# Letting a list scheduler overlap consecutive VectorE and ScalarE instructions in its model

## The chip, the cores and the metric

One core of one Trainium2 chip. The metric is the time of one execution on the device in microseconds (us). "Waits" of TensorE below are stretches in which TensorE could not start its next matmul; TensorE is the engine that sets the end of this kernel.

## The reference, cut to what matters

```python
def _attn_ref(q, k, v):                      # 4 batches, 8 heads, 768 tokens, head width 64
    k_sum = k.reshape(B, H, nb, 32, D).max(axis=3)      # block maxima of the keys
    v_sum = v.reshape(B, H, nb, 32, D).mean(axis=3)     # block means of the values
    # local scores inside a window of 16 tokens to each side, and scores against k_sum
    ...
    a = np.exp(scores_all); a = a / (np.sum(a, axis=-1, keepdims=True) + 1e-09)
    return np.matmul(a, np.concatenate([v, v_sum], axis=2))

def _moe_ref(x, w_gate, w1, w2):             # 3072 tokens, width 512, 8 experts, hidden 1024
    P = np.exp(x @ w_gate - ...)
    for _ in range(8):                       # Sinkhorn
        P /= P.sum(1, keepdims=True) + 1e-09; P /= P.sum(0, keepdims=True) + 1e-09; P *= N / E
    for e in range(E):
        out += P[:, e:e + 1] * (np.maximum(x @ w1[e], 0.0) @ w2[e])
```

## The kernel before

The kernel does the attention for 16 pairs of heads, 12 to 15 belonging to the last batch; between these it runs expert 0 on whatever tokens are ready, and then runs experts 1 to 7, with fewer and larger products (a Strassen-like scheme). So there are two stages: an attention stage to about 120 us, mixed with the products of expert 0, and an expert stage, in pure form from about 164 us to the end.

The order of all instructions on all engines comes from a list scheduler that runs while the program is being built. Each piece of work is a unit with an engine, a modelled cost, its dependences and a priority. On the chip each engine takes its instructions in just this order and waits at semaphores.

```python
class Plan:
    HOP = 0.15                                   # from one engine to another
    ...
    def order(self):
        ...
        while left:
            best = {}
            for u in left:
                ...
                for e, cost in u.eng.items():
                    t = max([t0, free.get(e, 0.0)]
                            + [d.end + d.lag + (self.HOP if d.on != e else 0.0) for d in u.deps])
                    best.setdefault(e, []).append((t, u, cost))
            for e, c in best.items():
                t_min = min(t for t, _, _ in c)
                t, u, cost = min((x for x in c if x[0] <= t_min + 0.02), key=lambda x: x[1].prio)
                picks.append((t, t + cost, e, u, cost))
            t, end, e, u, cost = min(picks, key=lambda x: x[:2])
            ...
            u.start, u.end, u.on = t, end, e
            free[e] = end
```

The 0.02 in the middle is a tie window: of the units that could start within 0.02 us of the earliest, the one of highest priority is taken.

The softmax here doesn't subtract the row's maximum and nothing guards it: scores larger than these inputs give would overflow.

## Time and profile before

| before | |
|---|---|
| median of the first three executions | 666.17 us (666.14 to 666.85) |
| span of the profiled execution | 664.1 us |
| TensorE waits that the view of waits shows, 17 to 164 us | none |
| hidden TensorE waits, 17 to 164 us (see below) | 0.61 us |

A matmul is drawn from its start to a modelled end: 379 ns for 512 columns, while in an unbroken stream the next one starts 216 ns after it. A wait of less than the difference, 163 ns, is covered by the drawn matmul, and the view of waits does not have it. So in all kernels of this study I measured hidden waits in one way: for every matmul that started 5 to 75 ns after the semaphore that it waited for was raised, the start-to-start time from the matmul before it, less the smallest such time of the same pair of kinds of matmuls in the traces of all kernels.

### The profile page before, as it was taken

How to read it: one execution, taken by the hardware profiler on the slowest of the kernel's cores; microseconds unless marked ns; L12 is line 12 of the kernel's file. 1: busy time of each engine (PE TensorE's matmuls, PEld its weight loads, DVE VectorE, ACT ScalarE, POOL GpSimd, SP SyncE). 2: the span in 40 equal slices, each digit the busy share in tenths (PEclk: the TensorE clock that was granted, in tenths of full speed). 3: DMA queues.
4: the chain of work that ended last, by engine and by line, in shares of the span. 5: the costliest groups of instructions: out<-in, count | busy, mean ns of one | idle time of the engine just before them, and what ended most of it. 6: DMA issues, size and time to landing. Idle time of an engine off the chain costs nothing.

```text
span 664.1 us, 13257 instructions
## 1 busy us (share of the span) xinstructions
PE 656.6 (99%) x5131; PEld 435.9 (66%) x5132; DVE 550.1 (83%) x1036; ACT 410.9 (62%) x769; POOL 199.0 (30%) x257
## 2 busy tenths in 40 slices
PE   8999999999999999999999999999999999999997
PEld 4666666545766666666666666666666666666666
DVE  7899897799988887887779877988778877988776
ACT  6677676556885566556665665555655656556652
POOL 8899522100132222212322222223122213222123
PEclk9999999999999999999999999999999999999999
DMA  9999932700953747373754665373838465335656
GB/s 167 181 145 145 143 70 43 128 1 2 157 96 65 126 75 118 64 128 65 110 97 71 121 91 101 64 127 65 127 64 135 73 96 96 64 64 112 157 134 202
DMA packets 112558, 67.89 MB, mean 102 GB/s; under 512 B 77936, under 2 KB 90480, under 8 KB 112496
## 3 DMA queue, kind: packets, MB, share of 16 engines
q0 software_dynamic: 94816, 57.46, 64.9%
q1 hardware_dynamic: 17152, 9.58, 5.9%
q8 instruction: 40, 0.66, 0.4%
q14 instruction: 22, 0.18, 0.1%
q10 hardware_dynamic: 528, 0.02, 0.0%
HBM read 52.45 MB, written 6.29 MB: 88 GB/s over the span
## 4 chain that ended last, share of the span: by engine, by line
PE 96%; DVE 3%; DMA 1%; issue 0%; ACT 0%; POOLq 0%; DVEq 0%
PE yps L815 22%; PE pA L764 22%; PE pY L815 17%; PE pQ L764 11%; PE hps L211 6%; PE yps L216 6%; PE pR L764 5%; PE sg L347 1%; DMA qst<-in_q_dram 1%; PE av L512 1%; PE vs L357 1%; PE tkq L303 1%; PE av L435 1%; DVE xs L543 1%; PE ss L461 1%; PE av L441 1%
## 5 line engine op out<-in xcount | busy, mean ns | idle before, releaser
L815 PEld LDWEIGHTS <-h 128*128 128x128 f16 x2352 | 230.1, 98 | 88.5 <-issue 1.0
L843 POOL DMA_DIRECT2D out_acc<-y x120 | 101.7, 891 | 372.1 <-ACT y L839 110.3
L839 ACT ACTIVATE y<-pY,P_sb 128x256 f32<-128x256 f32 x168 | 79.8, 477 | 123.3 <-PE pY L815 121.6
L830 DVE SCALAR_TENSOR_TENSOR out_acc<-yps,P_sb,out_acc 128x512 f32<-128x512 f32 x128 | 95.1, 744 | 29.0 <-PE yps L815 29.0
L798 DVE TENSOR_TENSOR h<-h 128x1024 f16<-128x1024 f16 x168 | 109.3, 683 | 1.4
L815 PE MATMUL pY<-w,h 128*128 128x256 f16 x672 | 100.0, 273 | 0.6 <-ACT y L839 0.6
L815 PE MATMUL yps<-w2sum,h 128*128 128x256 f16 x672 | 98.4, 273 | 0.0
L764 PE MATMUL pA<-xT,w 128*128 128x512 f16 x336 | 98.3, 379 | 0.0
L815 PE MATMUL yps<-w,h 128*128 128x256 f16 x672 | 93.3, 273 | 0.0
L830 DVE SCALAR_TENSOR_TENSOR out_acc<-pY,P_sb,out_acc 128x512 f32<-128x512 f32 x84 | 62.8, 748 | 29.1 <-PE pY L815 27.4
L764 PEld LDWEIGHTS <-w 128*128 128x128 f16 x672 | 65.8, 98 | 31.6 <-issue 0.2
L764 PEld LDWEIGHTS <-w1sum 128*128 128x128 f16 x504 | 49.3, 98 | 45.0
L786 DVE CUSTOM_DVE_ANT_0 h<-pQ,snap 128x512 f16<-128x512 f32 x84 | 57.6, 685 | 7.0 <-ACT snap L207 4.3
L786 DVE CUSTOM_DVE_ANT_0 h<-pA,snap 128x512 f16<-128x512 f32 x84 | 57.3, 682 | 4.8 <-PE pA L764 4.8
L202 ACT ACTIVATE h<-pA 128x512 f16<-128x512 f32 x84 | 50.6, 603 | 12.6 <-PE pA L764 12.4
L202 ACT ACTIVATE h<-pR 128x512 f16<-128x512 f32 x84 | 50.1, 596 | 8.0 <-PE pR L764 7.7
L207 ACT COPY pR<-pA 128x512 f32<-128x512 f32 x83 | 47.5, 572 | 7.7 <-PE pA L764 6.9
L815 PE MATMUL pY<-w2sum,h 128*128 128x256 f16 x336 | 50.4, 273 | 0.0
L764 PE MATMUL pA<-xsum,w 128*128 128x512 f16 x168 | 50.0, 379 | 0.0
L764 PE MATMUL pR<-xT,w 128*128 128x512 f16 x168 | 50.0, 379 | 0.0
L764 PE MATMUL pQ<-xsum,w1sum 128*128 128x512 f16 x168 | 50.0, 379 | 0.0
L764 PE MATMUL pA<-xsum,w1sum 128*128 128x512 f16 x168 | 50.0, 379 | 0.0
(150 smaller groups left out, 854.3 us busy)
## 6 DMA issues: line engine op xcount, KB each, us to landing
out_acc<-y POOLq DMA_DIRECT2D x120, 256.0 KB, 3.4
w<-in_moe_w_dram POOLq DMA_DIRECT2D x14, 1024.0 KB, 10.7
out_dram<-out_acc SPq DMA_DIRECT2D x24, 256.0 KB, 2.4
qst<-in_q_dram POOLq DMA_DIRECT2D x32, 96.0 KB, 5.3
vx<-in_v_dram POOLq DMA_DIRECT2D x15, 192.0 KB, 6.2
kst<-in_k_dram POOLq DMA_DIRECT2D x24, 96.0 KB, 5.6
w<-in_moe_w_dram POOLq DMA_DIRECT2D x4, 256.0 KB, 7.6
w<-in_moe_w_dram POOLq DMA_DIRECT2D x2, 512.0 KB, 7.7
```

Of the source, the lines that this page charges most:

```text
L202: nc.scalar.activation(out=out, in_=in_, func=AF.Relu, bias=0.0, scale=1.0)
L207: (nc.scalar.copy if eng == "ACT" else nc.vector.tensor_copy)(out=out, in_=in_)
L211: nc.tensor.matmul(hp[:, 0:n], lhsT=w1s[e][:, dk, f * 128:(f + 1) * 128], rhs=xT[:, dk, t0:t0 + n], start=(dk == 0), stop=(dk == KD - 1))
L216: nc.tensor.matmul(yp[:, d], lhsT=h[:, f, c * 128:(c + 1) * 128], rhs=w2s[e][:, f, d], start=(f == 0), stop=(f == KF - 1))
L303: nc.tensor.transpose(t[:, g * 128:(g + 1) * 128], st[:, g, :, :].rearrange("p j d -> p (j d)"), ident)
L764: nc.tensor.matmul(dst[:], lhsT=lhsT, rhs=rhs, start=first and k == 0, stop=k == HK - 1, skip_group_check=True)
L786: nc.vector._custom_dve(dve_ops.TENSOR_ADD_SAT, out=ring(e, p, q)[:, q % 2, blk, :], in0=at[src, e, p, q][:], in1=at.pop(("snap", n, e, p, ...
L798: nc.vector.tensor_tensor(out=h[:, :, out_, :], in0=h[:, :, a, :], in1=h[:, :, b, :], op=op)
L815: nc.tensor.matmul(dst[:, d], lhsT=lhsT, rhs=rhs, start=f == 0 and n in (1, 5, 2), stop=f == HF - 1, skip_group_check=True)
L830: nc.vector.scalar_tensor_tensor(out=o, in0=y, scalar=scalar, in1=o, op0=ALU.mult, op1=ALU.add)
L839: nc.scalar.activation(out=at[key][:, d], in_=src, func=AF.Copy, bias=0.0, scale=P_sb[:, t, e:e + 1])
L843: nc.gpsimd.dma_start(out=o, in_=at.pop(("y", e, p, c, key))[:], accum_op=ALU.add)
```

## The change

Its intent: recorded VectorE and ScalarE instructions overlap their successors by some 0.1 us, and a model that charges each its full recorded duration believes these engines to be slower than they are. With the overlap in the model the order should be better fitted to the chip.

```diff
     HOP = 0.15
+    OVERLAP = {"DVE": 0.07, "ACT": 0.09}
...
             u.start, u.end, u.on = t, end, e
-            free[e] = end
+            free[e] = end - self.OVERLAP.get(e, 0.0)
...
-    X_BY_DMA = 12
-    WHOLE = 10
+    X_BY_DMA = {12, 13, 14}
+    WHOLE = {10, 11, 12, 13, 14, 15}
...
-            rows = add("DVE", 1.65, sink_rows, prev, 0)
+            rows = add("DVE", 1.5, sink_rows, prev, 0)
```

(The tests `i >= WHOLE` become `i in WHOLE`, likewise for `X_BY_DMA`. The sets hold the pairs that the thresholds selected.)

More of the change, by code (lines that the diff above doesn't have):

```diff
@@ L384, in scores @@
             dst = [[sg[:, j, :] for j in range(2)], None]
-            if i >= WHOLE:
+            if i in WHOLE:
                 dst[1] = at["sg", i, 1] = [bank("a", "sg1") for _ in range(2)]
-            score_mms(i, dst, range(G if i >= WHOLE else HG))
+            score_mms(i, dst, range(G if i in WHOLE else HG))
         def scores_1(i):
@@ L948, in pair_whole @@
             deps = [U["kT", i, 0], U["kT", i, 1], U.get(("ed", i - 2))]
-            bufs = [Buffer("s")] + (2 * [None] if i < WHOLE else [Buffer("a"), Buffer("a")])
-            U["S", i, 0] = U["S", i, 1] = add("PE", 0.4 if i < WHOLE else 0.6, lambda: scores(i), deps, prio,
+            bufs = [Buffer("s")] + (2 * [None] if i not in WHOLE else [Buffer("a"), Buffer("a")])
+            U["S", i, 0] = U["S", i, 1] = add("PE", 0.4 if i not in WHOLE else 0.6, lambda: scores(i), deps, prio,
                                               opens=[x for x in bufs if x is not None])
             U["X", i, 0] = add("ACT", 0.97, lambda: score_exp(i, 0), [U["S", i, 0]], prio, uses=bufs[:1])
-            if i < WHOLE:
+            if i not in WHOLE:
                 buf = Buffer("s")
@@ L978, in pair_whole @@
                                     [U["A", i, h], U.get(("x", i - 2))], prio, uses=[buf])
-            if i >= X_BY_DMA and i % PB < PB - 1:
+            if i in X_BY_DMA:
                 U["xt", i] = add("SP", 1.5, lambda: x_dma(i), [U["no", i, 0], U["no", i, 1]], prio)
@@ L1100, in transposed @@
             nc.gpsimd.tensor_copy(out=warm[:, 1:2], in_=qT[r][0:32, W:W + 1])
-            if X_BY_DMA < NP:
+            if NP - 2 in X_BY_DMA:
                 nc.gpsimd.tensor_copy(out=warm[:, 4:5], in_=xT[0:32, PB - 2, (B - 1) * S:(B - 1) * S + 1])
@@ L1108 @@
         last[0] = add("POOL", 0.3, transposed, [last[0], U["near", NP - 1]] + [U["kT", NP - 1, z] for z in range(2)]
-                      + [U["x", i] for i in range(X_BY_DMA, NP - 1)])
+                      + [U["x", i] for i in X_BY_DMA])
         load("w1n", lambda: load_w1(1), 0.85, 5.0)
```

## The prediction

> **What bounds the kernel now.** I read the page first: busy shares, the 40 slices, the shares of the chain that ended last.
>
> ```profile
> span 664.1 us, 13257 instructions
> PE 656.6 (99%) x5131; PEld 435.9 (66%) x5132; DVE 550.1 (83%) x1036; ACT 410.9 (62%) x769; POOL 199.0 (30%) x257
> PE   8999999999999999999999999999999999999997
> DVE  7899897799988887887779877988778877988776
> PE 96%; DVE 3%; DMA 1%; issue 0%; ACT 0%; POOLq 0%; DVEq 0%
> ```
>
> TensorE is busy in 38 of 40 slices at full digits, and the last chain runs through it for 96% of the span. But the page warns that matmul ends are modelled: a matmul is drawn with its latency, so a wait shorter than that hides under the matmul before it. So I then read the chain in order of time, which is told by starts. One expert's period, from a start of the first of its products that the chain names to the same one an expert later:
>
> ```profile
> 312.29 0.86 PE pA L764 x4
> ...
> 385.23 0.86 PE pA L764 x4
> ...
> 458.17 0.86 PE pA L764 x4
> ...
> 531.10 0.86 PE pA L764 x4
> ...
> 604.04 0.86 PE pA L764 x4
> ```
>
> The periods are 72.94, 72.94, 72.93, 72.94 us. Per expert the code issues 12 groups of first-layer products (7 products of 2 matmuls, 168 matmuls) and 12 of second-layer products (7 of 4, 336 matmuls). The chain gives 0.86 us for four of the first and 0.87 for eight of the second: 42 x 0.86 + 42 x 0.87 = 72.7 us. That is the period within rounding (0.2 us), so the steady part, from about 164 us to 640, holds no wait of TensorE at all, even under the modelled ends. VectorE and ScalarE wait for TensorE there, not the reverse. The waits of TensorE alone, whole run:
>
> ```profile
> PE idle L613 <- DVE zeros L632: 1.3, 1, 1.3
> PE tkq L312 <- DMA qst<-in_q_dram: 0.8, 1, 0.8
> PE pY L815 <- ACT y L839: 0.6, 1, 0.6
> PE tkq L300 <- ACT kst L207: 0.3, 1, 0.3
> ```
>
> Three of the four come before 7 us, one in the last 7 us. For what hides under the latency I took, for each pair of neighbouring matmul kinds, the start-to-start time of every record above the smallest (for equal kinds, the lower quartile) of its kind. By five-microsecond stretches the surplus is 0.3, 1.3, 1.8, 1.0 (0 to 20 us), 1.3, 1.15, then about 0.4 each to 70 us, under 0.7 in any stretch to 110 us, 0.01 each from 115 to 640, and 0.18, 0.13, 0.01, 0.73 at the end. From 20 to 110 us the sum is about 7.5 us; most of it is a fixed pattern inside the score groups (steps of 66 and 77 ns between the two row halves, every time), which an order can't remove.
>
> The part at the end, in order of time:
>
> ```profile
> 655.63 1.75 PE yps L815 x16
> 657.38 0.45 PE pY L815 x4
> 657.83 0.02 issue
> 657.85 0.48 ACT y L839
> 658.33 0.04 issue
> 658.37 0.60 PE pY L815 x4
> 658.97 0.89 PE yps L815 x8
> ```
>
> The last product of one group waits for ScalarE to read the bank before it may add to it, and nothing is put between. Start to start of the matmul before and after it is 0.835 us against 0.109: 0.73 us lost.
>
> **What the Trainium skill says.** "Perfetto Trace Analysis", section Optimizing Scalar/DVE Operations: the second half of an instruction's profiled latency, the write acknowledgement, overlaps with the next instruction. The trace agrees: two neighbours on VectorE and two on ScalarE from the timeline at 300 us, in order of each engine:
>
> ```profile
> 300.17 0.60 ACT L202 ACTIVATE h<-pA 128x512 f16<-128x512 f32 x1 [0.17 <-PE pA L764]
> ...
> 300.66 0.59 ACT L202 ACTIVATE h<-pR 128x512 f16<-128x512 f32 x1
> ...
> 303.21 0.69 DVE L739 TENSOR_TENSOR w2sum<-w 128x1024 f16<-128x1024 f16 x1
> ...
> 303.82 0.68 DVE L786 CUSTOM_DVE_ANT_0 h<-pA,snap 128x512 f16<-128x512 f32 x1
> ```
>
> Starts are 0.49 apart for a 0.60 us instruction and 0.61 for a 0.69 us one: overlaps of 0.11 and 0.08. Over the whole trace 605 of 1035 neighbours on VectorE overlap, by 82 ns at the median, and 319 of 768 on ScalarE, by 103 ns. "VectorE: DVE Perf Modes", section The DRAIN you can't avoid, says that the next instruction does not start until the pipe empties; as a rule for recorded ends the trace differs, by those 82 ns. "TensorE: Matmul & The Clock Gate", section Step-by-step, gives 216 ns from one 512-column matmul to the next; here it is 0.86 / 4 = 0.215 us. "Perfetto Trace Analysis", section Optimization Strategy, says to look for the gaps on the most-contended engine: here only the first 110 and last 20 us have any.
>
> **The change, part by part.** (1) The scheduler that fixes every engine's program order before the run now calls VectorE free 0.07 us, ScalarE 0.09 us, before the modelled end. Modelled costs were full durations (sums of h: 0.69 against 683 ns; accumulation: 0.76 against 744; the relu: 0.60 against 603), so the old model overcharged every busy neighbour by the overlap, and the new numbers, below 82 and 103 ns, still overcharge a little. No instruction is removed or added; matmuls stay 5131. What can move is the order on each engine, and the engine of the copies that may run on either. (2) The two thresholds become sets, {12, 13, 14} and {10 to 15}; worked out by hand they select the same pairs as "from 12 on, except each batch's last" and "from 10 on" did. Cost 0. (3) The row part of the Sinkhorn loop is modelled 0.15 us shorter, 8 times 0.15 = 1.2 us of model time; its instructions are the same. (4) The order from 7 to about 20 us on TensorE, VectorE and ScalarE is a chain written by hand, which the scheduler must follow: cost 0.
>
> So the sum is over waits that an order could remove. 20 to 110 us: the two clear ones are a transposition of x at 20.2 us that starts 0.285 late after VectorE's normalization, and the logits at 65.9 us, 0.21 late; some five smaller ones of about 0.1; together 1.0. End: 0.73 + 0.17 + 0.12 = 1.0. At most 2.0 us, 0.3% of 666. In the steady 476 us the gain is 0: nothing waits. VectorE's modelled relief there, some 88 instructions x 0.07 = 6 us an expert, is off the path. I expect a quarter to a third of the 2.0 to be had, since an order that removes one of these can make another: -0.6 us.
>
> **The rivals.** (a) The order gains a lot because VectorE, 83% busy, becomes free earlier. Against: overlap on the chip was there before and is in the 666; the model alone learns of it, and 72.94 against 72.7 us leaves no room. It would need matmuls to vanish. 664.2 at best. (b) The tighter plan loses: a plan with less slack on VectorE puts dependent matmuls sooner behind it, and where the chip is later than the model TensorE waits. For: VectorE is busy 27.1 of 30 us from 20 to 50, and DMA is at its densest there, which the model knows only as constants. Against: the new overlaps are still smaller than measured. Two or three new waits of 0.3 to 0.5 us: 667.2. (c) Copies move to VectorE (now 43 of 168 snapshots), which would then be the bound in the steady part. In the old model VectorE is at about 90% there; the freed 6 us an expert would take up to 8 copies of 0.69 more, which leaves it where it was in the model and near 90% on the chip. A wait in every group of 12 x 7 would show as +0.1 x 84 = 8 us. I hold this for under 3%. (d) The end gets reordered: the second-half products could fill the 0.73 us hole, but the VectorE accumulation that they wait for ends at 658.46, no sooner than the ScalarE read at 658.33, so the hole only closes if that accumulation is also put ahead of another one: 0 to -0.7.
>
> **Range and chances.** Before ran 666.14 to 666.85, so 0.4 us is noise. From (a) and (d) downward about 2 us, from (b) upward about 1.2: predicted 665.6 us, 8 in 10 between 664.3 and 667.1. Faster by 2% is 13 us, more than all the waits of TensorE together: 1%. Slower by 2% needs (c): 1%. Within 2%: 98%.
>
> **What would show it right or wrong.** Right: an equal count of 5131 matmuls, periods of 72.9 us between equal starts of neighbouring experts, no TensorE wait between 164 and 640 us, the same chain to about 17 us, and a difference made of pieces under 1 us before 110 us and after 640. VectorE's busy time between 550 and 565 us, with more than 43 snapshots on it. Wrong: a period other than 72.9 (then (c)); a first expert product later or earlier than about 139.75 us, where it now starts, by over 2 us (then the attention stage mattered more than I read); a span that changes before 17 us (then the hand-written chain does not hold the order).

## More of the kernel before

The units of one later pair of heads on VectorE, with the costs in us that the model charges:

```python
# [cut from pair_start and pair_whole; only the VectorE units and the one DMA, for pairs 4 to 15]
U["kT", i, z] = add("DMA", 1.7, None, [U["tr", i, z]], prio, lag=2.0)          # pairs 12 to 15: keys transposed by DMA
U["kT", i, z] = add({"ACT": 0.8, "DVE": 0.56}, 0, ...tr_out...)                # pairs 4 to 11: copied out of PSUM
U["ks", i] = add("DVE", 0.95, lambda: key_max(i), [U["kT", i, 0], ...], prio)            # block maxima of the keys
U["km", i] = add("DVE", 0.23, lambda: key_max_split(i), [U["ks", i]] + ..., prio)
U["Vs", i] = add("DVE", 0.28 if i < PB else 0.7, lambda: block_out(i), [U["vs", i], sc], ...)   # two instructions
U["mk", i, h] = add("DVE", 0.56, lambda h=h: masks(i, h), ...)                           # twice a pair
U["ed", i] = add("DVE", 0.78, lambda: edges(i), ...)                                     # four instructions
U["no", i, h] = add("DVE", 0.75, lambda h=h: normalize(i, h), [U["A", i, h], ...])       # two instructions, twice a pair
```

A bank of PSUM that one of these reads (`vs` for the block sums, `av` for the attention products) can be filled again by TensorE only when it has been read. That is how VectorE being late becomes TensorE waiting.

## The result, and the profile after

Six executions of the changed kernel took 667.22 to 671.46 us, median 668.21; the kernel before on the same chip took 665.79 to 667.65, median 666.27. The ratio is 1.0033, with an interval of 1.0010 to 1.0057. (Ratios are the mean time of one kernel's fast executions over that of the other's of the same rounds, so not quite the ratio of the medians quoted.) Within 2%, but on the wrong side of the prediction, and outside its range.

The profiled execution was the slowest of the six, 671.46 us. The head of its page, as the prediction showed it of before:

```profile
span 669.7 us, 13281 instructions
...
PE 660.8 (99%) x5131; PEld 436.7 (65%) x5132; DVE 563.2 (84%) x1050; ACT 403.8 (60%) x755; POOL 198.9 (30%) x257
...
PE 92%; DMA 4%; POOL 3%; issue 0%; SPq 0%; DVE 0%; ACT 0%; POOLq 0%; DVEq 0%
```

The span is 5.6 us longer, the count of matmuls is the same, and VectorE has 14 instructions more, which ScalarE has less: 64 snapshots (copies of a PSUM bank that holds a partial sum) are now on VectorE where 43 were, and some copies of other kinds moved the other way. In the chain that ended last DMA has 4% and GpSimd 3%, where they had 1% and nothing. From the same view as in the prediction, the last chain in order of time, the equal starts of neighbouring experts:

```profile
340.67 0.86 PE pA L765 x4
...
413.61 0.86 PE pA L765 x4
...
486.55 0.86 PE pA L765 x4
```

The periods are 72.94 us, as before. So nothing was lost in the expert stage. The view of TensorE's waits, cut to 17 to 164 us, where before has none (us in total, times, longest):

```profile
PE av L442 <- DMA Ve<-vx: 0.9, 1, 0.9
PE av L436 <- DVE em L413: 0.9, 1, 0.9
...
```

Two waits of 0.9 us stand out, one ended by VectorE's masks (`em`), the other by a DMA. What VectorE did ahead of them, in order of time (start, duration, then the instruction and, in brackets, the idle time before it and what ended that):

```profile
75.92 0.56 DVE L205 TENSOR_SCALAR h<-hps 128x384 f16<-128x384 f32 x1 [0.31 <-PE hps L212]
79.65 0.95 DVE L336 TENSOR_REDUCE ks<-kT 128x24 bf16<-128x768 bf16 x1 [3.17 <-DMA kT<-kst]
...
82.23 0.55 DVE L413 TENSOR_TENSOR em<-er,band 128x768 bf16<-128x768 bf16 x1
```

VectorE stood still for 3.17 us, because the next instruction in its order was the block maxima of pair 12, and the keys of pair 12 were still being transposed by DMA. The masks of pair 10 (`em`, 82.23), whose input ScalarE had finished at 79.23, stood behind it and three more units in the order and could not pass. Then the masks were late for the attention products, and TensorE waited for them, the second wait in the view. The keys' transposition had been issued at 70.67 us and landed 9.0 us later; in the kernel before it was issued at 66.23, ahead of other transfers in its queue, and took 6.7.

The first wait in the view is not VectorE's. It ended when a transfer of neighbouring values (`Ve<-vx`) landed, which the chain of this execution follows:

```profile
76.12 7.91 DMA Ve<-vx
84.03 0.03 issue
84.06 0.52 PE av L442 x3
```

VectorE's edges for the same products ended only at 84.24 us, so that TensorE would have stood there for them too: two late paths met, and no run separates them.

The stall had an aftermath. The view of windows, with the granted clock as the third number from the right (then DMA share and GB/s), and the chain in the same place:

```profile
80.00:84.50 4.50, 2.46 (x27) 1.23 (x26) 4.10 (x11) 2.20 (x4) 0.00 (x0) 1.00 2.03 145
84.50:87.80 3.30, 3.30 (x14) 1.25 (x12) 2.17 (x4) 1.06 (x2) 0.00 (x0) 0.53 1.61 157
```

```profile
84.58 3.20 PE yps L217 x8
```

TensorE was busy 2.46 us of the 4.5 before 84.5 (its busy time is the second number), and for the next 3.3 us the granted clock was 0.53. The chain spends those in eight products of expert 0. Its 512-column matmuls there start 0.427 us apart where they otherwise start 0.216 apart; seven such steps cost about 7 x 0.211 = 1.5 us (an estimate). "TensorE: Matmul & The Clock Gate", Part 1 of the Trainium skill, has this state: half clock after an idle window of about 3.4 us, and 426.7 ns for 512 columns. The spacing agrees, and so does the length: the clock records of the trace have half clock from 84.67 us on for 3.41 us. The idle time that led to it was less than a whole window, 2.04 us in pieces.

So in this one execution these places account for most of the loss: waits of 0.38, 0.93, 1.03 and 0.17 us from 80.7 to 84.2 us, 2.5 together (the 1.03 is the one that a DMA ended), and 1.5 of slow clock: 4.0 of the 5.6 us between the two spans. But 671.46 us is not the typical time of this kernel. So the question for the experiments was whether this story holds for the five other executions.

### The profile page after: what moved, and what is told of

Read it like the earlier page. It is cut to its first block, busy times and chain, and to the rows that moved or that the text cites. A ratio compares the mean times of both kernels' runs of the same rounds, so it can differ in the third digit from the quotient of the medians.

```text
span 669.7 us, 13281 instructions
## 1 busy us (share of the span) xinstructions
PE 660.8 (99%) x5131; PEld 436.7 (65%) x5132; DVE 563.2 (84%) x1050; ACT 403.8 (60%) x755; POOL 198.9 (30%) x257
## 4 chain that ended last, share of the span: by engine, by line
PE 92%; DMA 4%; POOL 3%; issue 0%; SPq 0%; DVE 0%; ACT 0%; POOLq 0%; DVEq 0%
PE yps L816 22%; PE pA L765 22%; PE pY L816 16%; PE pQ L765 11%; PE yps L217 6%; PE pR L765 5%; PE hps L212 5%; DMA w<-in_moe_w_dram 1%; DMA Ve<-vx 1%; DMA vx<-in_v_dram 1%; PE av L442 1%; PE sg L348 1%; PE av L436 1%; PE vs L358 1%; POOL vx L290 1%; PE tkq L304 1%
## 5 line engine op out<-in xcount | busy, mean ns | idle before, releaser
L816 PE MATMUL yps<-w2sum,h 128*128 128x256 f16 x672 | 100.5, 273 | 0.0
L816 PE MATMUL yps<-w,h 128*128 128x256 f16 x672 | 90.5, 273 | 0.0
```

The costliest lines, as they stand in the source:

```text
L816: nc.tensor.matmul(dst[:, d], lhsT=lhsT, rhs=rhs, start=f == 0 and n in (1, 5, 2), stop=f == HF - 1, skip_group_check=True)
```

## The experiments

Eighteen runs were made, two of them repeats. Kernels are compared only within the same rounds. All computed the right result. The medians of before were 666.11 us in the first call, 666.00 in the second, 666.59, 666.31 and 666.27 in the following. The hidden waits are of each kernel's one profiled execution, 17 to 164 us, which need not be its median: it is the slowest of the run for the over-charged costs and the fastest for `HOP`.

### First theory: the late transposition of the keys stalls VectorE

**The changed kernel once more**, unchanged, for five rounds and a profile of a typical execution.

> The changed kernel once more, untouched, for its spread and for more than one profile. Late-transposition theory (VectorE's program has the block maxima of pair 12 just where the schedule thinks the transposed keys land; they land later, VectorE stands, the masks of pair 10 behind it are late, TensorE waits near 82 us and its clock drops for some us): 667.0 to 670, a wait of VectorE on the transposed keys of 1 to 4 us near 76 to 80 us in the profile, TensorE surplus of 1 to 4.5 us between 75 and 90 us. Lottery theory (a new order costs a bit everywhere): the same time, but no single stretch with more than 1 us in this profile.

It took 667.26 us (666.99 to 667.48) against 666.11: ratio 1.0017 (1.0004 to 1.0029). The profile:

```profile
span 665.7 us, 13281 instructions
...
PE 658.8 (99%) x5131; PEld 436.1 (66%) x5132; DVE 562.7 (85%) x1050; ACT 403.4 (61%) x755; POOL 198.9 (30%) x257
```

TensorE's busy time is 2.2 us longer than before for the same matmuls: a wait that the drawn length of a matmul covers counts as busy.

The view of TensorE's waits, 17 to 164 us, has one line for this execution:

```profile
PE vs L358 <- DVE xs L544: 0.2, 1, 0.2
```

No stall of 0.9 us, no slow clock, and still over 1 us lost. The hidden waits are 2.21 us, in eleven pieces of 0.09 to 0.38 us spread from 20 to 132 us, where before has three of 0.29, 0.08 and 0.21. One piece, seen from TensorE and from VectorE:

```profile
90.60 0.51 PE L358 MATMUL vs<-vx,m_blk 128*128 128x128 bf16 x6 [0.22 <-DVE xs L544]
```

```profile
89.99 0.56 DVE L544 TENSOR_TENSOR xs<-av,rc 128x384 f16<-128x384 f32 x1
```

The normalization on VectorE ends at 89.99 + 0.56 = 90.55 us and frees a bank; the block sums of another pair (`vs`), which take it, start at 90.60. The view gives 0.22 us of idle time; start to start against the smallest of that pair of kinds it is 0.38.

**The landing modelled later.** VectorE's head-of-line wait is there because the model lets the keys land 2.0 us after their 1.7 us on the queue. With 5.0 in its place the scheduler puts the block maxima later.

```diff
-  U["kT", i, z] = add("DMA", 1.7, None, [U["tr", i, z]], prio, lag=2.0)
+  U["kT", i, z] = add("DMA", 1.7, None, [U["tr", i, z]], prio, lag=5.0)
```

> The overlap of the change kept, the modelled landing of the four pairs of transpositions of keys and queries by DMA set 3 us later (2.0 to 5.0 us after the modelled transfer). The modelled end of the whole schedule stays the same. Late-transposition theory: the block maxima of pairs 12 to 15 stand 3.5 to 5.6 us behind the old modelled landing instead of 0.2, VectorE waits under 0.5 us for them, TensorE surplus between 75 and 90 us under 1 us, time 665.3 to 666.8. Lottery or overlap-itself theory: 667.5 to 669, like the changed kernel.

The wait is gone. VectorE's waits for keys from 60 to 95 us, first in the changed kernel:

```profile
DVE ks L336 <- DMA kT<-kst: 2.4, 3, 1.1
```

and with the later landing the same view has no such line; its longest are these:

```profile
DVE em L413 <- ACT er L409: 2.4, 5, 0.9
DVE kT L208 <- PE tkq L304: 1.1, 1, 1.1
```

Yet the time was 667.29 us, ratio 1.0018 (1.0006 to 1.0031): what VectorE had waited for was gone, and the time was that of the changed kernel. Hidden waits 1.65.

**Only the two blocked units moved.** In the changed kernel's order, the maxima of pair 12 go behind the edges of pair 10 on VectorE; nothing else moves.

```diff
-        for u in plan.order():
+        seq = plan.order()
+        late = [U["ks", 12], U["km", 12]]
+        seq = [u for u in seq if u not in late]
+        at_ = seq.index(U["ed", 10]) + 1
+        seq[at_:at_] = late
+        for u in seq:
```

> The changed kernel with only two VectorE instructions moved: the block maxima of pair 12 and their spread go behind the masks and edges of pair 10; every other engine keeps its order. Late-transposition theory: the wait of VectorE near 76 us ends or moves behind the edges, TensorE's surplus of 75 to 90 us falls to under 1 us, time 1 to 2 us below the changed kernel of this call (666 to 667.3). If the masks were late for another reason (the scores, or the neighbours' values by DMA): within 0.5 us of the changed kernel.

667.07 us, ratio 1.0018 (1.0004 to 1.0031). Its view of TensorE's waits:

```profile
PE tx L551 <- DVE xs L544: 0.6, 1, 0.6
...
PE ss L462 <- DVE Ve L364: 0.4, 1, 0.4
```

The waits moved: transpositions of x now wait 0.6 us for a normalization, and score products 0.4 for another VectorE unit that stood behind. Hidden waits 2.77.

**The clock kept up.** Eight idle matmuls of 512 columns in front of the attention products of pair 10 keep TensorE from standing still where the slow profile did.

```diff
         av = at["av", i, h] = bank("a", "av")
+        for _ in range(8 if (i, h) == (10, 0) else 0):
+            stream(av, 512)
```

> The changed kernel with eight idle matmuls of 512 columns (about 1.7 us at full rate) ahead of the values of pair 10, where TensorE stood, so that it isn't idle there. If the drop of the clock after the wait is a cost of its own: the profile shows no matmul at the double spacing of 0.43 us near 85 us, and where the wait is over 2 us the time falls by about 1.5 us against the changed kernel; where the wait is short, the fill itself costs up to 1.7 us. Net against the changed kernel of this call: -1 to +0.7 us, and less spread. If the clock drop costs nothing: +0.5 to +1.7 us.

668.38 us, ratio 1.0034 (1.0021 to 1.0046). Eight matmuls cost 8 x 0.216 = 1.73 us, and hidden waits fell to 1.27. The stall did not come in this kernel's profile or, by its range (668.29 to 668.62), in any of the five executions, so that this run says nothing about the clock. It is inconclusive for what it was made for.

The first theory falls. It describes part of the slow execution; the typical loss is there without that stall.

### Second theory: the full charge was a hidden margin, and the overlap is not the same in both stages

The timeline of VectorE in the kernel before, inside the attention stage, tells how units follow each other there:

```profile
70.34 0.18 DVE L542 RECIPROCAL rc<-av 128x6 f32<-128x6 f32 x1
70.56 0.56 DVE L543 TENSOR_TENSOR xs<-av,rc 128x384 f16<-128x384 f32 x1
71.03 0.28 DVE L363 TENSOR_TENSOR Ve<-vs,own_n 64x128 bf16<-64x128 f32 x1
71.34 0.48 DVE L367 COPY Ve<-Ve 64x650 bf16<-64x650 bf16 x1
...
72.46 0.19 DVE L420 TENSOR_TENSOR Ee<-er,band 32x80 bf16<-32x80 bf16 x1
72.66 0.20 DVE L424 TENSOR_TENSOR Ee<-er,band 32x80 bf16<-32x80 bf16 x1
72.87 0.19 DVE L420 TENSOR_TENSOR Ee<-er,band 32x80 bf16<-32x80 bf16 x1
73.09 0.20 DVE L424 TENSOR_TENSOR Ee<-er,band 32x80 bf16<-32x80 bf16 x1
73.32 0.56 DVE L204 TENSOR_SCALAR h<-hps 128x384 f16<-128x384 f32 x1
```

Take start plus duration of each line against the next start. Inside a normalization (70.34 and 70.56) the product waits for the reciprocal: 70.52 to 70.56, a gap of 0.04. From 70.34 to 71.12 it takes 0.78 us; the model charges 0.75. The next unit does overlap it, starting at 71.03, 0.09 us before its end. The block sums of the values (71.03 and 71.34) have a gap inside too: 0.79 us, charged 0.70. The four pieces of the edges (72.46 to 73.09) follow each other without any overlap: 0.83 us, charged 0.78, and the next instruction, at 73.32, starts after their end.

Over the whole trace of before:

| neighbours without idle time between them | mean overlap | pairs that overlap |
|---|---|---|
| VectorE units, 20 to 120 us | 0.047 us | 96 of 135 |
| VectorE units, 164 to 640 us | 0.075 us | 416 of 437 |
| VectorE, inside one unit, 20 to 120 us | none: a gap of 0.027 us | |
| ScalarE, 20 to 120 us | 0.051 us | 41 of 68 |
| ScalarE, 164 to 640 us | 0.080 us | 250 of 312 |

So 0.07 us is right for the expert stage and too much for the attention stage. An estimate for one later pair of heads, of about ten VectorE units: the units' costs leave out 2 x 0.028 (normalizations) + 0.095 (block sums) + 0.054 (edges) = 0.205 us, and have 0.04 too much in masks and split; so the old model charged 10 x 0.047 - 0.165 = 0.31 us too much, and the new one charges 10 x (0.07 - 0.047) + 0.165 = 0.40 us too little.

This can be read directly. The scheduler's modelled start of each block maxima and each normalization can be listed and set against its start in the trace. The mean of chip less model, in us, by modelled time:

| kernel | 18-40 | 40-60 | 60-80 | 80-100 | 100-120 |
|---|---|---|---|---|---|
| before | -0.33 | -0.23 | -0.96 | -1.35 | -2.05 |
| changed (typical execution) | -0.06 | 0.19 | 0.23 | 0.68 | 0.48 |
| changed (slow execution) | 0.19 | 0.88 | 1.35 | 4.23 | 4.51 |

Before, the chip ran ahead of the model by up to 2 us. After, it runs behind the model. This is no lead of VectorE over TensorE: TensorE's block sums (`vs`), set against the model in the same way, moved with it (before -0.92 and -1.33 at 60 to 100 us, changed 0.07 and 0.57). So the table says that the whole stage ran faster, and then slower, than modelled, and TensorE's new waits may be the cause of the second as well as its result. The theory: the old overcharge was a margin that nobody had put there on purpose, and the change took it away in the attention stage. Its rivals: a new order is simply a new draw, some orders are better and this one is worse; or ScalarE's overlap does it; or the margin is wanted between engines, not on VectorE.

**A margin elsewhere.** The change, with 0.25 us in place of 0.15 for a hand-over from engine to engine (`HOP`).

> The change kept, but the scheduler charges 0.25 us instead of 0.15 for every handover from one engine to another. The scheduler's own end grows from 666.7 to 668.8 us. Lost-margin theory (VectorE's and ScalarE's overcharge was the margin that kept TensorE from waiting on the chip; the margin can come from anywhere): hidden waits of TensorE from 17 to 164 us fall from 2.0 us (the changed kernel repeated) to under 1.0, time 665.5 to 666.4. Lottery theory (every new order costs some waits, whatever the margin; the kernel before is one that was tuned by hand): 666.5 to 668.5, waits of 1 to 3 us. Schedule's-own-end theory: 668 or more.

667.08 us (666.54 to 672.15), ratio 1.0028 (1.0007 to 1.0050). The chip ran ahead of this model (-0.48 to -1.46 us), and hidden waits were 1.38 in the profiled execution, the fastest (666.54 us); yet the median stayed 1.1 us above before. One execution of the six, at a clock of 0.994, took 672.15 and widens the ratio; the other five average 667.05, against 666.19 for before. This counts against the theory in its simple form: being ahead of the model is not enough.

**ScalarE alone**, `OVERLAP = {"ACT": 0.09}`.

> Overlap for ScalarE alone, VectorE charged in full as before. Lost-margin theory, with VectorE, the busier engine (27 of 30 us from 20 to 50), as the one that matters: 665.8 to 666.6, hidden waits from 17 to 164 us under 1.0 us. Lottery theory: 666.5 to 668.5.

666.50 us against 666.00, ratio 1.0008 (0.9996 to 1.0020). The chip stays ahead of the model (-0.68 at 80 to 100 us), hidden waits 0.68 and 0.56 more after 164 us.

**VectorE alone**, `OVERLAP = {"DVE": 0.07}`.

> Overlap for VectorE alone. Lost-margin theory: like the changed kernel, 667.0 to 668.0, hidden waits from 17 to 164 us 1.2 to 3 us. Lottery theory: 666.5 to 668.5. Both overlaps needed together: 666.0 to 666.6.

667.37 us, ratio 1.0025 (1.0013 to 1.0038), hidden waits 2.04, chip behind the model (0.73). It is VectorE's overlap that costs.

**Another order without any overlap**, the kernel before with a tie window of 0.01 us.

> The kernel before with no overlap at all; only the window in which the scheduler calls two candidates equal goes from 0.02 to 0.01 us. The margin stays whole and the order of TensorE up to 164 us changes for about a third of the units. Lost-margin theory: 665.8 to 666.6, hidden waits from 17 to 164 us under 1.0 us. Lottery theory: 666.5 to 668.5 with waits of 1 to 3 us, as for any new order.

666.50 us, ratio 1.0010 (0.9998 to 1.0022), hidden waits 1.16, over the expected 1.0. A new order alone can cost about 0.5 us: the order of before is a good one among its like.

**The change with honest costs.** Cost less 0.07 is made the start-to-start time that measured duration and mean overlap (0.047) give: normalization 0.80, block sums 0.30 and 0.82, edges 0.86, maxima 0.97, masks 0.57.

```diff
-  U["no", i, h] = add("DVE", 0.75, ...        +  0.80
-  U["Vs", i] = add("DVE", 0.28 / 0.7, ...     +  0.30 / 0.82
-  U["ed", i] = add("DVE", 0.78, ...           +  0.86
-  U["ks", i] = add("DVE", 0.95, ...           +  0.97
-  U["mk", i, h] = add("DVE", 0.56, ... (whole pairs)   +  0.57
```

> The change's overlaps kept, but VectorE's own costs in the attention stage set to what the traces show there: normalization 0.80 for 0.75, summary of values 0.82 for 0.70, edges 0.86 for 0.78, block maxima 0.97, masks 0.57 (so that cost less 0.07 is the measured time less the measured mean overlap of 0.047 between units in that stage). Wrong-sign theory (the 0.07 holds between long instructions of the expert stage; in the attention stage it turns an overcharge of some 0.26 us a pair into an undercharge of 0.42, the chip falls behind the plan, and TensorE waits): hidden waits from 17 to 164 us under 1.0, VectorE within 0.3 us of the plan from 40 to 100 us, time 665.9 to 666.6. Margin theory (an overcharge is needed, a true charge isn't enough): 666.5 to 667.3. Lottery: 666.4 to 668 with no relation to the charge.

666.97 us (666.44 to 667.92) against 666.59, ratio 1.0005 (0.9993 to 1.0018). The loss is no longer clear of noise. But the hidden waits of its profile are 1.77, one of them 0.75 us behind a relu on VectorE, and the chip still fell behind the model by 0.62 at 80 to 100 us: that part of the expectation missed.

**The same costs and 0.05 us more on each.**

> As the run with the measured costs, each of the five costs another 0.05 us higher: VectorE overcharged in the attention stage again, the overlaps kept. Wrong-sign theory and margin theory: 665.8 to 666.6, hidden waits from 17 to 164 us under 1.0 us, the chip 0.5 to 2 us ahead of the plan by 100 us. Lottery: 666.4 to 668.

666.63 us against 666.59, ratio 0.9998 (0.9984 to 1.0012). The chip is ahead of the model again (-0.45 at 80 to 100). Of its 1.42 us of hidden waits 1.18 lie before 22 us and are put down to a DMA of weights (0.61) and a ScalarE copy (0.57), not to VectorE. The waits missed the expected 1.0. But with the change in place and VectorE's attention units charged fully, the loss is gone.

**The change with another order** (tie window 0.01).

> The change kept, the window of equal candidates 0.01 us instead of 0.02: another order from the same overlaps, its own modelled end the same 666.7 us. Wrong-sign and margin theory: like the changed kernel, 667.0 to 668.2, hidden waits from 17 to 164 us 1.3 to 3 us, the chip behind the plan by 0.3 to 1.2 us from 60 to 100 us. Lottery: 666.0 to 668.

668.09 us (667.79 to 668.39) against 666.59, ratio 1.0021 (1.0008 to 1.0033), with one wait of 1.28 us at 82 us behind a normalization. A different order, the same loss.

**Before with a wide tie window** (0.04).

> The kernel before with a window of 0.04 us: a second new order without overlap; its modelled end is 675.5 us, 7.5 above that of before. Wrong-sign and margin theory: 665.8 to 666.8, hidden waits from 17 to 164 us under 1.2 us, the chip several us ahead of the plan. Lottery: 666.4 to 668. Schedule's-own-end theory: 672 or more.

670.95 us, ratio 1.0064 (1.0051 to 1.0077): the worst of all, without any overlap in its model. Here the model itself said so: its modelled end was 675.5 us against 667.95 for before, with 6.6 us of modelled gaps on TensorE after 164 us, and the chip had 3.03 us of waits there. This missed what the theory had expected (665.8 to 666.8), and that the model foresaw it was seen only afterwards. An order can lose in other ways.

### The decisive pair: overlap in one stage only, in two orders each

The overlap holds only for units whose modelled end is before 120 us ("early"), or only from there on ("late"); each with the tie window of 0.02 and with 0.01.

```diff
-  free[e] = end - self.OVERLAP.get(e, 0.0)
+  free[e] = end - (self.OVERLAP.get(e, 0.0) if end < 120.0 else 0.0)      # early; late: end >= 120.0
```

> Half of the change: the overlaps apply only where the modelled end is under 120 us, which is the attention stage. Wrong-charge theory (the loss comes from the undercharge in the attention stage alone): 1.0015 to 1.0035 times before, hidden waits from 17 to 164 us 1.5 to 3 us. If the expert stage's new order were the cause: 0.9995 to 1.0010.

> The other half: the overlaps apply only from a modelled end of 120 us on. Wrong-charge theory: 0.9990 to 1.0010 times before, hidden waits from 17 to 164 us under 1.0 us. If the expert stage's new order were the cause: 1.0015 or more.

> Overlaps in the attention stage alone, with another order of it (window of equal candidates 0.01 us). Wrong-charge theory: 1.0015 to 1.0035 again, waits 1.5 to 3 us. Lottery theory: no relation to its partner without the other window, 0.999 to 1.003.

> Overlaps from 120 us on alone, with the other window, so another order of the attention stage under the full charge. Wrong-charge theory: 0.9995 to 1.0012, waits from 17 to 164 us under 1.2 us. Lottery theory: 0.999 to 1.003.

| | median, us | less before (666.31) | ratio | hidden waits, us |
|---|---|---|---|---|
| early | 666.96 | +0.65 | 0.9997 (0.9970 to 1.0023) | 2.29 |
| early, tie 0.01 | 668.03 | +1.72 | 1.0006 (0.9979 to 1.0033) | 1.83 |
| late | 665.95 | -0.36 | 0.9983 (0.9956 to 1.0010) | 0.58 |
| late, tie 0.01 | 666.34 | +0.03 | 0.9984 (0.9956 to 1.0013) | 1.18 |

Three of the eleven executions of before in this call took 669.6 to 670.7 us at a granted clock of 0.995 to 0.996; they raise its mean, so all four ratios are too low and their intervals wide. Against each other the medians are clear, since all four ran in the same rounds: in either order, the early half costs 1.0 to 1.7 us more than the late half, and the hidden waits follow. (By their ratios both early kernels missed the expected 1.0015 to 1.0035.) With tie 0.01 the two do not even touch (666.79 to 668.43, and 666.27 to 666.57). The chip's lead over the model at 80 to 100 us has the theory's sign: 1.03 and 0.69 behind in the early kernels, 1.12 and 0.90 ahead in the late ones.

What this pair decides is the stage. It adds no new order of that stage: the scheduler's order up to 120 us of model time is that of the changed kernel in "early" and that of before in "late", on every engine, and with tie 0.01 that of the two tie 0.01 kernels above.

**The late half again**, to see whether it beats both kernels.

> The overlaps from 120 us of model time on alone, once more, since its median was the lowest of all kernels. Wrong-charge theory: 0.9985 to 1.0008 times before; a gain over before, if there is one, is under 0.1% (its order up to 164 us is nearly that of before, with 0.5 us of hidden waits).

665.78 us (665.77 to 666.44) against 666.27, ratio 0.9993 (0.9981 to 1.0005). Its view of TensorE's waits from 17 to 164 us is empty, as that of before is, and the hidden ones are the same three: 0.29, 0.07 and 0.22. The medians of both calls are 0.4 and 0.5 us under before, but neither interval leaves out 1. It is no worse, and perhaps 0.1 us of it has a known place: the wait at the end is 0.90 us in its hidden waits, 1.02 in before. It is the best version.

**The over-charged costs in another order** (tie window 0.01).

> The overlaps everywhere, VectorE's five costs of the attention stage corrected and 0.05 us more, in a second order (window 0.01 us). Wrong-charge theory: 0.9990 to 1.0012 times before, hidden waits from 17 to 164 us under 1.3 us. Lottery theory: 0.999 to 1.003.

666.63 us against 666.27, ratio 1.0015 (0.9996 to 1.0034); one execution of six took 670.50 at a clock of 0.995. So in a second order, too, the loss is not clear of noise, though the ratio lies just above the expected 1.0012.

### All runs side by side

| kernel | VectorE overlap in the attention stage at the old costs | median less that of before, us | hidden waits | interval of the ratio leaves out 1 |
|---|---|---|---|---|
| changed (the six executions) | yes | +1.94 | 3.86 | yes |
| changed, again | yes | +1.15 | 2.21 | yes |
| later landing | yes | +1.18 | 1.65 | yes |
| two units moved | yes | +0.96 | 2.77 | yes |
| idle matmuls | yes | +2.27 | 1.27, and 1.73 of fill | yes |
| hop 0.25 | yes | +1.08 | 1.38 | yes |
| VectorE alone | yes | +1.37 | 2.04 | yes |
| changed, tie 0.01 | yes | +1.50 | 2.91 | yes |
| early | yes | +0.65 | 2.29 | no (outliers of before) |
| early, tie 0.01 | yes | +1.72 | 1.83 | no (outliers of before) |
| ScalarE alone | no | +0.50 | 0.68, and 0.56 later | no |
| before, tie 0.01 | no | +0.50 | 1.16 | no |
| late; again | no | -0.36; -0.49 | 0.58; 0.59 | no |
| late, tie 0.01 | no | +0.03 | 1.18 | no |
| honest costs | corrected | +0.38 | 1.77 | no |
| over-charged | corrected | +0.04 | 1.42 | no |
| over-charged, tie 0.01 | corrected | +0.36 | 1.36 | no |
| before, tie 0.04 | no | +4.36 | 2.40, and 3.03 later | yes |

Seven kernels with VectorE's overlap in the attention stage at the old costs ran where the kernel before had none of the outliers of 669 us and more: the changed one and six variants. All seven are above before with an interval that leaves out 1 (one of them, with the idle matmuls, mostly by its own 1.73 us). Of the nine runs without it or with corrected costs only the one whose own model was 7.5 us worse is. These are fewer orders than runs: up to 120 us the rows with "yes" hold five (the changed one, which "two units moved" alters by two units on VectorE and "later landing" from 76 us on; hop; VectorE alone; tie 0.01), the others seven.

Splitting the hidden waits of at least 0.06 us by the engine whose semaphore came last (a fresh count from the traces, so not to the hundredth the sums above) gives VectorE 0.65 to 2.29 us in the rows with "yes" (1.58 of 2.13 in the typical changed execution), 0.19 to 0.78 in those with "no", 0.13 and 0.14 with over-charged costs, but 1.35 with honest costs. With the later landing and the idle matmuls VectorE's part is 0.88 and 0.65, near the 0.64 of before: the waits that they have beyond it ended at ScalarE, DMA or TensorE's own work.

What is shown: the loss comes with VectorE's overlap in the attention stage, in several orders; it goes when the overlap is kept to the expert stage or when VectorE's attention units are charged more; it lies in short TensorE waits, most of them behind VectorE. What is argued from the table of chip less model, and not shown as a law: that the sign of this difference decides, or that the overcharge worked as a margin. The kernel with hop 0.25 was ahead of its model and lost 1.1 us all the same, and honest costs missed their waits. And up to 0.5 us of any such difference is the draw of the order: the two orders without any overlap in the attention stage differ by 0.4 to 0.5 us.

Open: why the transposition and the neighbouring values landed so late in the slow execution; what the other slow executions are (the kernel before has them too, 669.6 to 670.7 us at a clock of 0.995 to 0.996, and none of these was profiled); and what the slow clock costs by itself.

## Why the prediction was right or wrong

**Right.** The matmuls are 5131, the periods 72.94 us, no wait stands between 164 and 640 us; the sets changed nothing; the wait at the end in front of the last `pY` group stayed (0.6 us in the view of waits before and after), as the working of its rival (d) suggested; VectorE's busy time is 563.2 us, in the stated 550 to 565, with 64 snapshots. Rivals (a) and (c) did not happen, and the class, within 2%, is right. One of its signs of error was set on a misread line: 139.75 us is where a list of the chain's longest pieces first names a product of expert 1, but the first one starts at 127.78. It moved to 128.95 in the typical execution, within the 2 us that were set, and to 132.98 in the slow one. The attention stage mattered more than the prediction read.

**Wrong: the step "I expect a quarter to a third of the 2.0 to be had, since an order that removes one of these can make another: -0.6 us".** The waits to be gained were sized a little high (0.61 us from 17 to 164 us where it had 1.0, and 1.02 at the end where it had 1.0), but the waits to be made were not sized at all. What was had: the one at 65.9 us, 0.21, and 0.12 at the end. What was made: in the typical execution ten new waits between 48 and 133 us, 1.84 together. Net: 2.21 - 0.61 = 1.60 in that stretch, and the span rose from 664.1 to 665.7.

**Why it was not sized: the clause of part (1), "the new numbers, below 82 and 103 ns, still overcharge a little".** 82 ns is the median of only those neighbours that overlap, over the whole trace, and the expert stage gives most of these. In the attention stage, where the waits of this change lie, the mean over all neighbours is 47 ns and units of several instructions are charged too little. The model went from an overcharge to an undercharge. A number was taken from one stage and used in another.

**The rival that came true was (b), "the tighter plan loses", with "two or three new waits of 0.3 to 0.5 us: 667.2".** Its kind of loss, short TensorE waits behind VectorE, is what the runs show. The clause that weakened it, "Against: the new overlaps are still smaller than measured", is the same error. Its size was near for the typical execution (667.26 us), in part by luck, with ten shorter waits in place of two or three; it had no term for a stall like that of the slow execution (2.5 us of waits and 1.5 us of slow clock).

**The reading of the Trainium skill.** The prediction cited "VectorE: DVE Perf Modes", section The DRAIN you can't avoid, and dismissed it by its 82 ns. That section sends the reader on to another, Two Vector instructions with no wait between them: a next instruction starts early only if it is not held, and one is held when its operands start at another quarter of the partitions than those before it. The four edge pieces, whose inputs start at partitions 0, 96, 0 and 96, agree: 0.01 to 0.03 us between each end and the next start, no overlap. (No run here varies the partitions alone, so the cause of these gaps is the page's.) Read to its end, it would have said that the overlap is a matter of which instructions follow each other, and sent me to count by stage.

## What to carry to other kernels

When a cost model that fixes an order is made more exact, measure the correction in the stage where the order can matter, as the mean over all neighbours and not the median of those that show the effect; check in the trace whether the chip then runs ahead of the plan or behind it. A plan that charges a little too much is a margin, and to take it away in a stage where the bounding engine is fed closely can cost more than the better order brings. The slowest execution tells a vivid story of its own: profile a typical one before explaining the median.

## What the Trainium skill lacked or had wrong

- "Perfetto Trace Analysis", Optimizing Scalar/DVE Operations, tells of the overlap as a property of every instruction. Here it depends on the neighbours: on VectorE a mean of 0.075 us (416 of 437 overlap) in the expert stage, 0.047 us (96 of 135) in the attention stage, and a gap of 0.027 us inside units whose second instruction depends on or is held by the first.
- "VectorE: DVE Perf Modes", The DRAIN you can't avoid, says that the next instruction does not start until the pipe empties, and in the same paragraph that one that is not held starts earlier. It is not wrong here, but it gives no size: among the neighbours on VectorE that overlap, the recorded start lies 0.08 us before the recorded end of the one ahead at the median, as at 71.03 us in the timeline of before (0.09).
- No page says how to find TensorE waits that the drawn length of a matmul hides. "TensorE: Matmul & The Clock Gate", Single matmul latency and Back-to-back issue gap, has both parts of it, as formulas: a warm latency that comes to 379 ns for 512 columns and an issue gap that comes to 216 ns, which the trace shows as well. What follows is that waits of up to 163 ns are invisible; of the eleven in the typical execution, 2.21 us, the view of waits shows one, of 0.2 us.
- The same page, Back-to-back issue gap, gives about 131 ns per 512-column matmul as the sustained rate of a stream of weight loads and matmuls. In this kernel, where each matmul has its weight load, the spacing is 216 ns (0.86 us for four).
- The same page, Part 1, ties the half clock to an idle window of about 3.4 us. Here it came after 2.04 us without matmuls in 4.5, and lasted 3.41 us at 0.5 by the clock records. It was seen in the middle of one profile only.
